# Transposed q and k copied out of PSUM in halves for every pair, in a fused window-attention and mixer kernel

## The chip, the cores and the metric

The kernel runs on one core of a Trainium2 chip. The metric is the device time of one execution in microseconds (us), given as the median over several runs. TensorE is called PE in the profile, VectorE DVE, ScalarE ACT, GpSimd POOL and SyncE SP.

## The reference, cut to what matters

Windowed attention with four sink tokens is followed by a mixer block over tokens and channels. There are 4 batches, 8 heads, 768 positions and head size 64; the mixer's widths are 256 (tokens) and 1536 (channels).

```
scores = scale * np.matmul(q, k.transpose(0, 1, 3, 2))
keep = is_sink | in_window          # first 4 keys, or 0 <= query - key < 128
a = softmax(np.where(keep, scores, -1e9))
x = matmul(a, v)                    # heads side by side: [4, 768, 512]
h = np.maximum(xt @ w_tok1, 0.0) @ w_tok2      # xt: x with tokens last
u = x + h.transpose(0, 2, 1)
out = u + np.maximum(u @ w_ch1, 0.0) @ w_ch2
```

## The kernel before, in words

Work comes in 16 pairs of heads, p = 0 to 15, four of them a batch (`NHP = 4`). For one pair:

- `prepare(p)` (line 393) makes the instructions that copy transposed q and k from PSUM to SBUF, and `transposed(p)` (line 447) is the burst of 24 small PE transposes that fills the PSUM tile they read. The tile has the tag "sc"; its first index x, 0 or 1, separates the first half of the 768 columns from the second, and both q and k have a part in each half. For pairs 0 to 4 q and k are copied in two halves of 384 columns each, from tiles of the tag "mx" (`turn`, line 429). For pairs 5 to 15 each is one copy of 768 columns from the "sc" tile.
- `cleared` (line 470) then zeroes a part of that tile for its next use, on DVE.
- `scores(p, g)` (line 499) multiplies q and k for three groups g, ACT takes the exponential (line 539), and DVE applies a mask (line 547).
- `sink_values(p)` (line 628) opens two PSUM tiles of the tag "mx", one for each head i, and `values(p, i)` (line 662) adds the window's part with 11 matmuls a head. `recip` and `norm` (lines 645 to 653) divide by the sum, both on DVE, and so empty the tile.

For a batch the mixer runs `mix_h` and `mix_u` (tokens), `turned_u` (transposes of u) and `mix_channels` (channels). In `mix_channels` a unit `v1` is four matmuls of 384 columns with w_ch1 into one "mx" tile, emptied by a relu on ACT or DVE (lines 135 and 137), and a unit `out_part` is three matmuls of 512 columns with w_ch2; four of these share one "mx" tile, which is emptied by an addition on DVE (line 924).

PSUM has two tiles of the tag "sc" and four of the tag "mx" (`TAGS`, line 68). A unit on PE that needs a tile takes the one that its readers left first.

The order of all instructions is written out ahead of time by a planner (`Plan`, line 247). PE takes the channel mixing of batch b as its main list, and the attention and token mixing of batch b+1 as a side list. `MERGED` (line 47) gives the merge by hand: "28/48" means that the side list's unit 28 comes once 48 units of the main list are placed. The planner then places the copies, relus and other work on ACT and DVE at the moment at which its own costs say an engine can begin them. Where two of them can begin at the same moment on the same engine, the one with the larger `urgent` goes first, and otherwise the earlier one in the list. In this planner a copy out of PSUM depends on the transposes and on who used its destination before. The planner does not know that one PSUM tile is read by one engine at a time: the tile framework adds such a wait between ACT and DVE by itself when the program is built.

Loads of q, k and v are issued by POOL (lines 107 and 115), stores of the output by SP (line 930).

Of the kernel before, what the change touches and what calls it, by code (L numbers as in the profile page):

```python
# [16 lines left out]
def kernel(  # L17
# [23 lines left out]
    NHP = H // 2  # L41
# [3 lines left out]


    MERGED = (
# [5 lines left out]
    )  # L53
    NQ = 6
    NPT = 3
# [18 lines left out]
    def bank(tag, *shape, dtype=FP32, slot=None):  # L74

        n = given[tag].pop(0) if slot is None else slot
        if tag == "sc":
            return sc[n]
        return psum.tile([P, *shape], dtype, name=f"ps_{tag}", tag=f"{tag}{n}", bufs=1)
# [41 lines left out]
    def mm(*args, **kwargs):  # L121
        in_order(nc.tensor.matmul(*args, skip_group_check=True, **kwargs))  # L122
# [4 lines left out]
    def copy(e, out, in_):  # L127
        if e == "ACT":
            in_order(nc.scalar.activation(out, in_, AF.Copy))  # L129
        else:  # L130
            in_order({"DVE": nc.vector, "POOL": nc.gpsimd}[e].tensor_copy(out=out, in_=in_))  # L131
# [10 lines left out]
    done = {}  # L142
    tiles = {}
# [50 lines left out]
    for n in range(4):  # L194
        i, odd = n // 2, n % 2
# [190 lines left out]
    def piece(ns, fn, deps, need, then, keys=()):  # L386
        op = Op({}, fn, deps, then, size=float(ns))
        op.need, op.keys = need, keys
        return op
# [3 lines left out]
    def prepare(p):  # L393

        kT = kTb[p % NKB]
        parts = 2 if p <= NHP else 1

        def evict(e, n, part):
            name = ("q", "k")[n]
            if n:  # L400
                t = kT
            elif ("qT", p) in tiles:
                t = tiles["qT", p]
            else:
                t = tiles["qT", p] = att_pool.tile([P, S], BF16, name="qT2")
            to = t.rearrange("d (x p j) -> d x p j", x=2, j=NT)
            copy(e, to if parts == 1 else to[:, part], tiles["ps_" + name, p] if parts == 1 else tiles["ps_" + name, p][part])

        free = ([("sk", p - 2)] if p >= 2 else [], [(n, p - NKB) for n in ("s", "sk")] if p >= NKB else [])
        if parts == 2:  # L410
            cost = {"DVE": 540.0, "ACT": 500.0}
        else:
            cost = {"DVE": 950.0} if p < NHP else {"DVE": 950.0, "ACT": 900.0}
        for n, name in enumerate(("qT", "kT")):
            done[name, p] = [
                Op(dict(cost), lambda e, n=n, part=part: evict(e, n, part), free[n]) for part in range(parts)
            ]
            for part, op in enumerate(done[name, p]):
                op.urgent = (3 - part) * (p < NHP)
        tiles["kT", p] = kT  # L420
# [26 lines left out]
    def transposed(p):  # L447

        def run():
            ps = turned_bank(p)  # L450
            for n in range(2):
                for j in range(NT):
                    for x in range(2):
                        rows = ds(D * x, D)
                        in_order(nc.tensor.transpose(ps[:, x, n, j], bfs[p, n][rows, j], ident[rows, rows]))  # L455
                tiles["ps_" + "qk"[n], p] = ps[:, :, n].rearrange("d x j p -> d x p j")

        then = [*done["qT", p], *done["kT", p]]
        then.append(cleared(p, then))
        return piece(  # L460
            350, run, [done["q_bf", p], done["k_bf", p]], {"sc": [then]}, then, [("tq", p), ("tk", p)],
        )

    def turned_bank(key):

        tiles["ps_turned", key] = bank("sc")
        t = tiles["ps_turned", key].bitcast(BF16).rearrange("d x n b c -> d x n (b c)")[:, :, :, 2 * D:8 * D]
        return t.rearrange("d x n (j p) -> d x n j p", j=NT)

    def cleared(key, readers):  # L470

        op = Op(
            {"DVE": 400.0}, lambda e: in_order(nc.vector.memset(tiles["ps_turned", key][0:D, :, :, 3], 0.0)), readers,
        )
        op.urgent = 2
        return op
# [151 lines left out]
    def sink_values(p):  # L628

        b, hp = pairs[p]  # L630
        vsk = v_sinks[p % NHP]

        def run():
            for i in range(2):
                tiles["ps_o", p, i] = bank("mx", NT, D1)
            for qt in range(2, NT):
                for i in range(2):
                    rows = ds(D * i, D)
                    mm(
                        tiles["ps_o", p, i][:, qt], tiles["pT_sink", p][rows, ts(qt - 2, P)], vsk[rows, i],  # L640
                        start=(qt == 2), stop=False,
                    )

        for i in range(2):
            def recip(e, i=i):
                r = tiles["recip", p, i] = pt_pool.tile([P, NT, 1], FP32, name="recip")
                in_order(nc.vector.reciprocal(r, tiles["ps_o", p, i][:, :, D:D1]))

            def norm(e, i=i):
                in_order(nc.vector.tensor_tensor(  # L650
                    out=x_sb[b][:, :, ds((2 * hp + i) * D, D)], in0=tiles["ps_o", p, i][:, :, 0:D],
                    in1=tiles["recip", p, i].to_broadcast([P, NT, D]), op=ALU.mult,
                ))

            done["r", p, i] = Op({"DVE": 180.0}, recip)
            done["x", p, i] = Op({"DVE": 550.0}, norm, [done["r", p, i]])
            done["r", p, i].urgent = done["x", p, i].urgent = 3
        return piece(
            120, run, [done["p", p, NT], done["vs", p]], {"mx": [[done[n, p, i] for n in "rx"] for i in range(2)]}, [],
        )  # L660
# [185 lines left out]
    def attention_and_tokens():  # L846

        parts, units = [], []
        first, last = NHP, len(pairs) - 1
        prepare(first)  # L850
        units += [turn(first, n) for n in range(2)]
        for p in range(first, last + 1):
            b, hp = pairs[p]
            pieces = []
            if p < last:
                prepare(p + 1)
                pieces.append(transposed(p + 1))
            pieces.append(scores(p, 0))
            if p > first:
                pieces.append(sink_values(p - 1))  # L860
            if p == last:
                pieces.append(turned_u(b, 0, "sc"))
            units.append(burst(*pieces))
            if p > first:
                units += [values(p - 1, i) for i in range(2)]
            pieces = [scores(p, 1), scores(p, 2)]
            if hp == 0 and p > first:
                units.append(mix_h(b - 1, 1, 0, NTOK))
                units += [mix_u(b - 1, 1, st, 2) for st in range(0, NT, 2)]
                pieces.append(turned_u(b - 1, 1))  # L870
            if hp == NHP - 1 and p < last:
                pieces.append(turned_u(b, 0))
            if hp % 2 == 0:
                pieces.append(score_sinks(p + 1))
            units.append(burst(*pieces))
            units[-1].then.append(sink_rows(p))
            if hp == 2:
                units.append(mix_h(b, 0, 0, NTOK))
                units += [mix_u(b, 0, st, 2) for st in range(0, NT, 2)]
            if hp == 0 and p > first:  # L880
                parts.append(units)
                units = []
        units += [pv(p, half) for half in range(2)]
        units.append(mix_h(b, 1, 0, NTOK))
        units += [mix_u(b, 1, st, 2) for st in range(0, NT, 2)]
        units.append(burst(turned_u(b, 1)))
        return parts + [units]
# [166 lines left out]
    parts = attention_and_tokens()  # L1054
# [40 lines left out]
```

## Time and profile before

| | us |
|---|---|
| median of 3 runs (lowest to highest) | 206.93 (206.88 to 207.99) |
| the profiled execution | 206.41 |
| its span, first to last instruction | 204.6 |
| PE busy | 197.6 (97%) |
| ACT busy | 113.8 (56%) |
| DVE busy | 112.4 (55%) |
| POOL busy | 67.3 (33%) |
| mean granted PE clock | 1.00 |

The profiled execution is 1.8 us longer than the span of its instructions. A busy share counts the time in which at least one instruction of an engine ran; matmuls are pipelined, so PE's share is high even where it pauses for a few tenths of a microsecond. What limits PE from moment to moment is seen in the order of time, in the stretch of the timeline around a wait.

### The profile page before, as it was taken

The page shows a single profiled execution, that of the slowest core. Times are in us where ns is not written, and L with a number is a line of the kernel's source. Part 1 is how long each engine was busy: PE and PEld are TensorE (multiplying, and loading weights), DVE is VectorE, ACT ScalarE, POOL GpSimd, SP SyncE. Part 2 cuts the span into 40 slices and gives each one's busy share as a digit, 9 for nine tenths or more (in the row PEclk, how much of TensorE's full clock was granted, in tenths as well). Part 3 has the DMA queues.
Part 4 walks back from the last instruction along what each step waited for, and adds up shares of the span by engine and source line. Part 5 has one row for each costly group of instructions (what it writes and reads, how often), then busy time and mean ns, then how long its engine had stood idle before and what let it go on. Part 6 is the DMA issues. An engine that isn't in the chain of part 4 may idle for free.

```text
span 204.6 us, 5496 instructions
## 1 busy us (share of the span) xinstructions
PE 197.6 (97%) x2377; PEld 119.3 (58%) x2377; DVE 112.4 (55%) x238; ACT 113.8 (56%) x195; POOL 67.3 (33%) x86
## 2 busy tenths in 40 slices
PE   6798999999999999999999999999999999999994
PEld 2345985566665665667656545666655645665453
DVE  4775653657788766866948557572654361001222
ACT  4898668879706535886563145886750114773000
POOL 6299859795699891450000000000000000000000
DMA  6999999999999999193001112100002112000223
GB/s 193 292 257 188 169 177 191 160 172 206 157 180 189 187 184 198 22 128 20 3 0 54 53 64 97 51 5 0 0 3 103 51 54 103 0 3 0 103 103 103
DMA packets 73223, 21.58 MB, mean 105 GB/s; under 512 B 63216, under 2 KB 70256, under 8 KB 73200
## 3 DMA queue, kind: packets, MB, share of 16 engines
q0 software_dynamic: 67232, 11.80, 73.1%
q1 hardware_dynamic: 5968, 9.45, 13.1%
q8 instruction: 18, 0.29, 0.6%
q14 instruction: 5, 0.04, 0.1%
HBM read 26.75 MB, written 6.29 MB: 161 GB/s over the span
## 4 chain that ended last, share of the span: by engine, by line
PE 85%; DMA 6%; DVE 3%; ACT 2%; POOL 1%; issue 1%; SPq 0%; POOLq 0%; ACTq 0%
PE ps_mx L122 77%; PE ps_sc L122 4%; DMA w_tok<-in_moe_w_tok_dram 4%; DMA v_sink_f<-in_v_dram 2%; PE ps_sc L455 2%; POOL v_aug L115 1%; DVE kT L131 1%; PE ps_mx L427 1%; ACT pT L539 1%; ACT qT L129 1%; PE ps_mx L125 1%; SPq L197 0%; ACT uT L129 0%; DVE u_sb L751 0%; DVE x_sb L650 0%
## 5 line engine op out<-in xcount | busy, mean ns | idle before, releaser
L122 PE MATMUL ps_mx<-uT,w_ch 128*128 128x384 bf16 x384 | 67.1, 326 | 0.1
L122 PE MATMUL ps_mx<-w_ch,v1T 128*128 128x512 bf16 (+2 forms) x312 | 66.9, 363 | 0.0
L539 ACT ACTIVATE pT<-ps_sc 128x1024 bf16<-128x1024 f32 (+1 forms) x48 | 44.4, 952 | 13.0 <-PE ps_sc L122 12.9
L122 PEld LDWEIGHTS <-w_ch 128*128 128x128 bf16 x384 | 36.0, 98 | 23.9 <-issue 1.2
L135 ACT ACTIVATE v1T<-ps_mx 128x384 bf16<-128x384 f32 x77 | 37.7, 490 | 19.5 <-PE ps_mx L122 18.9
L122 PEld LDWEIGHTS <-v1T 128*128 128x128 bf16 x312 | 28.3, 98 | 27.6 <-issue 0.5
L924 DVE TENSOR_TENSOR o_sb<-ps_mx,u_sb 128x512 f32<-128x512 f32 x23 | 15.8, 687 | 34.6 <-PE ps_mx L122 34.6
L122 PEld LDWEIGHTS <-w_tok 128*128 128x128 bf16 x192 | 18.3, 98 | 5.9 <-DMA w_tok<-in_moe_w_tok_dram 0.7
L107 POOL DMA_DIRECT2D q_bf<-in_q_dram x24 | 19.6, 822 | 4.4 <-DMA w_ch<-in_moe_w_ch_dram 2.2
L107 POOL DMA_DIRECT2D k_bf<-in_k_dram x24 | 19.6, 820 | 4.1 <-DMA w_ch<-in_moe_w_ch_dram 1.7
L751 DVE TENSOR_TENSOR u_sb<-ps_mx,x_sb 128x512 bf16<-128x512 f32 x20 | 13.2, 687 | 13.0 <-PE ps_mx L122 12.9
L115 POOL DMA_DIRECT2D v_aug<-in_v_dram x16 | 16.4, 1026 | 8.3 <-ACT v_sink L129 7.1
L131 DVE COPY kT<-ps_sc 128x768 bf16<-128x768 bf16 x11 | 10.5, 958 | 13.4 <-ACT qT L129 13.4
L122 PEld LDWEIGHTS <-pT 128*128 128x128 bf16 x352 | 14.1, 98 | 3.3 <-issue 0.6
L129 ACT ACTIVATE qT<-ps_sc 128x768 bf16<-128x768 bf16 x11 | 8.9, 810 | 12.3 <-PE ps_sc L455 12.1
L122 PE MATMUL ps_mx<-v_aug,pT 128*128 128x65 bf16 x352 | 15.6, 194 | 0.0
L547 DVE TENSOR_TENSOR pT<-pT,mask_main 128x1024 bf16<-128x1024 bf16 (+1 forms) x24 | 14.3, 619 | 1.3 <-ACT pT L539 1.3
L122 PE MATMUL ps_sc<-qT,kT 64*64 64x192 bf16 (+3 forms) x288 | 14.4, 248 | 0.0
L135 ACT ACTIVATE h1T<-ps_mx 128x512 bf16<-128x512 f32 (+1 forms) x8 | 4.1, 517 | 17.1 <-PE ps_mx L122 16.9
L122 PE MATMUL ps_mx<-h1T,w_tok 128*128 128x256 bf16 x96 | 13.2, 273 | 0.0
L137 DVE TENSOR_SCALAR v1T<-ps_mx 128x384 bf16<-128x384 f32 x19 | 10.4, 549 | 4.9 <-PE ps_mx L122 4.9
L122 PE MATMUL ps_mx<-x_sb,w_tok 128*128 128x256 bf16 x96 | 12.0, 273 | 0.5 <-DMA w_tok<-in_moe_w_tok_dram 0.4
(68 smaller groups left out, 156.6 us busy)
## 6 DMA issues: line engine op xcount, KB each, us to landing
out_dram<-o_sb SPq DMA_DIRECT2D x23, 256.0 KB, 2.0
v_aug<-in_v_dram POOLq DMA_DIRECT2D x16, 192.0 KB, 7.2
w_ch<-in_moe_w_ch_dram POOLq DMA_DIRECT2D x8, 384.0 KB, 8.8
q_bf<-in_q_dram POOLq DMA_DIRECT2D x24, 96.0 KB, 6.8
k_bf<-in_k_dram POOLq DMA_DIRECT2D x24, 96.0 KB, 5.9
q_f<-in_q_dram SPq DMA_DIRECT2D x4, 384.0 KB, 5.0
k_f<-in_k_dram SPq DMA_DIRECT2D x4, 384.0 KB, 5.7
w_tok<-in_moe_w_tok_dram POOLq DMA_DIRECT2D x2, 384.0 KB, 7.7
```

The lines of the kernel that those rows point to most:

```text
L107: in_order(nc.gpsimd.dma_start(out=out[:, h], in_=rows[:, h]))
L115: in_order(nc.gpsimd.dma_start(out=v_aug.rearrange("p i t d -> p (i t) d")[:, :, 0:D], in_=v[b].rearrange("h s d -> (h s) d")[2 * hp * S:2 ...
L122: in_order(nc.tensor.matmul(*args, skip_group_check=True, **kwargs))
L129: in_order(nc.scalar.activation(out, in_, AF.Copy))
L131: in_order({"DVE": nc.vector, "POOL": nc.gpsimd}[e].tensor_copy(out=out, in_=in_))
L135: in_order(nc.scalar.activation(out, in_, AF.Relu))
L137: in_order(nc.vector.tensor_scalar_max(out=out, in0=in_, scalar1=0.0))
L455: in_order(nc.tensor.transpose(ps[:, x, n, j], bfs[p, n][rows, j], ident[rows, rows]))
L539: in_order(nc.scalar.activation(part(tiles["pT", p][:, :, ds(2 * g, 2)]), of_keys(tiles["ps_s", p, g])[:, :, 0:width(g)], AF.Exp, scale=scale,
L547: in_order(nc.vector.tensor_tensor(out=pt, in0=pt, in1=m, op=ALU.mult))
L751: in_order(nc.vector.tensor_tensor(out=u_part(b, g, s0, n), in0=tiles["ps_u", b, g, s0], in1=x_sb[b][:, s0:s0 + n, c0:c0 + cn], op=ALU.add,))
L924: in_order(nc.vector.tensor_tensor(out=o_sb.rearrange("p (g c) -> p g c", g=2), in1=u_rows(b, st), in0=tiles["ps_out", b, st].rearrange("p ...
```

## The change

Three edits. First, the copies of transposed q and k are made in two halves of 384 columns for all pairs, where pairs 5 to 15 had one copy of 768 columns each. Second, `transposed` hands out the two halves of its PSUM tile one by one. Third, the order number `urgent` of the reciprocal and the normalisation in `sink_values` is 2 in place of 3, which is the number that `cleared` has. The list `MERGED` is another one, with the same 75 units of the side list.

```
     MERGED = (
-        "1/0 0/2 2/4 3/8 4/15 5/17 6/17 7/19 8/24 9/25 10/25 11/27 12/27 13/29 14/29 15/30 16/32 17/32 18/35 "
-        "19/36 20/38 21/38 22/38 23/41 25/42 26/42 24/42 27/44 28/48 29/50 31/52 30/52 32/56 33/57 34/57 "
-        "35/60 36/61 39/63 40/63 41/65 42/67 38/67 37/67 43/71 44/76 45/76 46/76 47/80 50/82 48/82 49/82 "
-        "51/86 52/92 53/95 54/95 55/95 56/100 57/102 58/102 59/105 60/106 62/115 67/115 63/115 61/118 64/120 "
-        "65/121 66/128 68/130 69/131 70/133 71/135 72/135 73/135 74/138"
+        "0/0 1/3 2/5 3/10 4/17 5/17 6/18 7/21 8/24 9/25 10/26 11/27 12/28 14/30 13/30 15/31 16/32 17/33 18/34 "
+        "19/36 20/39 21/39 22/39 23/41 26/42 25/42 24/42 27/44 28/51 29/52 30/53 31/55 32/60 33/60 34/60 "
+        "35/65 36/65 37/68 38/68 39/69 40/72 41/73 42/75 43/75 44/80 45/80 46/80 47/83 48/85 49/86 50/86 "
+        "51/88 52/94 53/97 54/97 55/97 56/102 57/103 58/103 60/108 59/110 63/114 61/115 62/115 64/119 67/124 "
+        "65/127 68/129 66/129 69/130 70/133 73/137 71/137 72/138 74/142"
     )
...
     def prepare(p):
...
-        parts = 2 if p <= NHP else 1
+        parts = 2
...
-                tiles["ps_" + "qk"[n], p] = ps[:, :, n].rearrange("d x j p -> d x p j")
+                tiles["ps_" + "qk"[n], p] = [ps[:, x, n].rearrange("d j p -> d p j") for x in range(2)]
...
-            done["r", p, i].urgent = done["x", p, i].urgent = 3
+            done["r", p, i].urgent = done["x", p, i].urgent = 2
```

## The prediction, made before the changed kernel ran

> **What bounds the kernel now.** I read the page's busy shares first, then PE's waits, then the groups of instructions by shape, then the timeline around one pair, and last the chain that ended last.
>
> ```profile
> PE 197.6 (97%) x2377; PEld 119.3 (58%) x2377; DVE 112.4 (55%) x238; ACT 113.8 (56%) x195; POOL 67.3 (33%) x86
> ```
>
> PE is busy for 97% of the span at a granted clock of 1.00 in every stretch, and the two copying engines for little over half. A change that leaves PE's matmuls alone can save only pauses of PE, and can add some. Consecutive matmul starts that lie over 0.1 us further apart than usual, and are not one of PE's regular changes between 64-row and 128-row work, occur after 30 us at four places alone: 70.13 (0.21 us), 72.31 (0.20), 89.86 (0.10) and 98.36 (0.23), 0.74 us together. So little can be won; the question is what new pauses come.
>
> The rows of the copies, with their single durations and what DVE waited for:
>
> ```profile
> L131 DVE COPY kT<-ps_sc 128x768 bf16<-128x768 bf16 x11 | 10.5, 958 | 13.4 <-ACT qT L129 13.4
> L129 ACT ACTIVATE qT<-ps_sc 128x768 bf16<-128x768 bf16 x11 | 8.9, 810 | 12.3 <-PE ps_sc L455 12.1
> L129 ACT ACTIVATE kT<-ps_mx 128x384 bf16<-128x384 bf16 x6 | 2.9, 505 | 0.7 <-PE ps_mx L439 0.6
> L129 ACT ACTIVATE qT<-ps_mx 128x384 bf16<-128x384 bf16 x6 | 2.8, 489 | 0.8 <-PE ps_mx L439 0.6 <-ACT pT L539 0.2
> L131 DVE COPY qT<-ps_mx 128x384 bf16<-128x384 bf16 x4 | 2.2, 554 | 1.2 <-PE ps_mx L439 1.1
> L131 DVE COPY kT<-ps_mx 128x384 bf16<-128x384 bf16 x4 | 2.2, 553 | 1.1 <-PE ps_mx L439 1.1
> L650 DVE TENSOR_TENSOR x_sb<-ps_mx,recip 128x384 bf16<-128x384 f32 x22 | 11.5, 549 | 0.1
> ```
>
> The first row carries the argument: for all 11 pairs k's copy on DVE waits for q's copy on ACT, though it needs nothing of it. The two engines read one PSUM tile in turn. The timeline of pair 6 shows the same in order of time (start, duration):
>
> ```profile
> 42.92 0.28 PE L122 MATMUL ps_mx<-v_sink,pT_sink 64*128 64x65 bf16 x8
> 42.97 0.81 ACT L129 ACTIVATE qT<-ps_sc 128x768 bf16<-128x768 bf16 x1
> 43.14 1.47 PE L122 MATMUL ps_mx<-uT,w_ch 128*128 128x384 bf16 x8
> 43.81 0.96 DVE L131 COPY kT<-ps_sc 128x768 bf16<-128x768 bf16 x1 [2.10 <-ACT qT L129]
> 44.00 0.49 ACT L135 ACTIVATE v1T<-ps_mx 128x384 bf16<-128x384 f32 x1 [0.22 <-PE ps_mx L122]
> 44.38 1.02 ACT L539 ACTIVATE pT<-ps_sc 128x1024 bf16<-128x1024 f32 x1
> 44.45 0.83 PE L122 MATMUL ps_mx<-v_aug,pT 128*128 128x65 bf16 x22
> 45.12 1.46 PE L122 MATMUL ps_mx<-uT,w_ch 128*128 128x384 bf16 x8
> ```
>
> From here come the sizes used below. A unit of four w_ch1 matmuls takes (44.45 - 43.14)/2 = 0.65 us; 11 matmuls of `values` take (45.12 - 44.45)/2 = 0.34; w_ch1 begins 0.17 after ACT's first copy. The hand-off from ACT to DVE is 43.81 - 43.78 = 0.03. Two independent instructions on ACT or DVE overlap by about 0.1 and 0.08 us. And in the chain, the pause at 98.36 is this copy's queue too: q, k, the zeroing and a relu, one after the other, until PE goes on 0.06 us after the relu.
>
> ```profile
> 96.05 0.82 ACT qT L129
> 96.90 0.97 DVE kT L131
> 97.86 0.11 issue
> 97.97 0.27 DVE ps_sc L473
> 98.25 0.46 DVE v1T L137
> ```
>
> **The change part by part.** *PE's work.* The built program has the same 2377 matmuls, and the same 74 changes between 64-row and 128-row work: no term. POOL's list is the same and SP stores in the same order, so transfers move only as PE's steps do, and POOL is idle after 90 us. Up to 30 us all engines' lists agree.
>
> *The halves.* The built program still lets one engine at a time read the tile. Its waits make a chain of four: ACT copies q's first half, DVE waits for it and copies q's second, ACT waits for that and copies k's first half, and DVE waits again and copies k's second. (For pairs 9, 11 and 13 ACT makes both halves of k.) By the rows: 0.49 + 0.55 + 0.51 + 0.55 and three hand-offs of 0.03 make 2.19 us, where 0.81 + 0.03 + 0.96 = 1.80 stood. The chain ends 0.39 us later, and engine time rises by 0.18 us a pair on ACT and 0.15 on DVE, 2.0 and 1.6 us over 11 pairs, which engines that are 56% busy hide. What costs is the place in the queue: ACT's instruction for k now stands ahead of exponential and relus and waits for DVE, and DVE's stands ahead of the normalisation and waits for ACT. Scores themselves do not wait, as those of the pair come several us later.
>
> *The merge.* What matters is how many "mx" tiles PE needs before these queues give one back. `sink_values` holds two of the four until the normalisation; w_ch1 units take one each 0.65 us. Under w_ch2 four units share a tile for 2.6 us, so pairs 7, 8, 9, 12 and 13 have cover; pair 14 has two such units first; pair 5 has no `values` open; at pair 11 the second k half is not on DVE and normalisation goes early. There remain pairs 6, 10 and 15. Before, two w_ch1 units went ahead of `values` there, and ACT's relu right after q's copy (44.00 to 44.49) gave the first tile back in time. Now only one or none goes ahead, and that relu stands behind k's half and the exponential.
>
> With zero at the start of q's first half: DVE q to 1.07, ACT k to 1.61, DVE k to 2.19.
> - Pair 6: `values` 0.17 to 0.51, a unit to 1.16, `values` to 1.50, a unit to 2.15, and the third unit needs a tile at 2.15. The normalisation (0.55, after k's half on DVE, overlap 0.08) ends at 2.66; ACT's exponential (1.02) and relu (0.49) end at 2.92. PE resumes at 2.66 + 0.06 = 2.72: **0.57 us**.
> - Pairs 10 and 15: a unit, both `values` and a second unit, then a third at 2.15, which gets the first unit's tile (relu right behind k on ACT, to 2.00). The fourth wants one at 2.80. DVE after k: reciprocal 0.17, zeroing 0.27 (begins 0.12 after the copy, as at 97.97), normalisation 0.55, overlapping 0.08 each where independent: 3.05, and PE at 3.11: **0.30 us each**.
>
> Bounds: with no hand-offs and each copy at 0.49 to 0.55 the three sum to about 0.9; with 0.12 at each hand-off, the largest such gap in the rows (the zeroing behind k), 0.27 more at each of three places, 2.0. I take 1.17, since the 0.03 of ACT to DVE is the same kind of step.
>
> *What goes.* The pause at 98.36 (pair 12) falls under w_ch2 now, and the one at 89.86 (pair 11) has both `values` and so the normalisation earlier: 0.33 us saved; by the bounds between 0 and 0.33. Those at 70.13 and 72.31 wait for a normalisation and a relu of token mixing, and the order there is nearly the same: 0, from -0.2 to +0.1.
>
> *`urgent`.* With 2 in place of 3 a normalisation and a zeroing that could begin together go in list order; in the built lists the zeroing (0.27) goes ahead of one at pairs 10 and 15, which is in their sum. At pair 6 it goes behind.
>
> Sum: 0.57 + 0.60 - 0.33 = +0.84 us. The profiled execution would take 206.41 + 0.84 = 207.25; the median shown lies 0.52 above it, so the median would be 207.8. About 0.5%, 1.0 us, is what a measurement of this kernel can tell from no change, and the forecast stays just inside it.
>
> **The rivals.**
> - *Halves side by side.* If the two halves of the tile were read at once, ACT's q with DVE's q and then k likewise, the chain would end at 2 x 0.55 + 0.03 = 1.14 in place of 1.80, the normalisation at pair 6 at 1.6, before 2.15, and no new pause comes: 206.93 - 0.33 and at most 0.4 for the other two places, 206.2 to 206.6, not slower. It decides when k's second half on DVE ends before 1.6. For it: the halves are separate parts of the tile. Against it: the 13.4 us of waiting behind ACT, and the same waits between halves in the built program. The Trainium skill, "PSUM — Partial Sum Buffer", section on PSUM bank collisions, says that ScalarE and VectorE may use different banks at once and need guarding by bank (and quadrant) alone; by that rule such waits are not needed between halves in different banks, and the time would be this rival's. The trace does not show two such reads at once.
> - *More places pause.* The layout leaves PE little room elsewhere: pairs 5, 11 and 14 meet w_ch1 units too, and a step from DVE back to ACT inside a tile has no row. At 0.12 a step and two or three places more of 0.3: 0.84 + 0.8 + 0.6, so 208.3 to 209.2. For it: ACT's queue now waits in the middle at eight pairs. Against it: ACT and DVE are idle over 40% of the time.
> - *Nothing to see.* DVE and ACT catch up sooner than laid out, since the planner may have placed relus on the other engine: pauses of 0.3 as gone, 206.6 to 207.1.
>
> **How the numbers follow.** Forecast 0.59 (207.2 to 208.3, centre 207.8; of this 0.11 lies above 207.96), halves side by side 0.07, more places 0.24, nothing to see 0.10. Under 205.9, faster by over 0.5%, lies part of the first rival with an error in the other pauses: 0.05. Slower by over 0.5%: 0.11 + 0.24 = 0.35. Between them: 0.48 + 0.10 + 0.02 = 0.60. The range reaches from the middle of the first rival, 206.5, to 208.9 inside the second.
>
> **What would show it.** In the changed profile: DVE's q and k halves each idle behind ACT and ACT's k half behind DVE, 2.2 us from the first start to the last end; at pairs 6, 10 and 15 (near 46, 85 and 136 us) PE held by the normalisation for 0.6, 0.3 and 0.3 us; no pause at pair 12. The forecast is wrong if halves of ACT and DVE overlap in time, if a copy of 384 columns from the "sc" tile takes much longer than 0.49 to 0.55 us, or if PE is held at other pairs.

## The result, and the profile after

The changed kernel takes 207.74 us (median of 22 runs, 207.00 to 208.93), and the kernel before, run beside it as often, 206.99 (206.11 to 208.12). The ratio is 1.0033, 95% interval 1.0019 to 1.0047: 0.75 us by the medians, slower by less than the 0.5% of the forecast's bound. The interval, 0.4 to 1.0 us, does not hold zero, so the slowdown is real though small. The forecast was 207.8.

The profiled execution of the changed kernel took 208.09 us, with a span of 206.3 and a granted clock of 0.998. Against 206.41 that is 1.68 us more, twice what the medians differ by. Half of it has nothing to do with the change: up to the last of the 128-row transposes of the first batch's u, all engines' lists are the same, and that one starts at 30.03 us before and at 30.82 after, 0.79 us of scatter between two executions. From there to the end the kernel before takes 174.61 us and the changed one 175.49: **+0.88 us**. This stretch is used for all comparisons of traces below.

The busy shares after, from the page:

```profile
PE 198.2 (96%) x2356; PEld 120.0 (58%) x2377; DVE 109.0 (53%) x240; ACT 118.5 (57%) x215; POOL 67.3 (33%) x86
```

Nothing changed its place as the bound. The 2377 weight loads are there; 21 of the matmuls have left no record, so a gap in the matmuls counts as a pause only where the weight loads or a waiting row show it too. The copies from the "sc" tile after, among the groups of instructions by shape (count, then busy us, mean ns of one, then idle time before them and what ended it):

```profile
L129 ACT ACTIVATE kT<-ps_sc 128x384 bf16<-128x384 bf16 x14 | 6.5, 490 | 6.9 <-DVE qT L131 6.9
L131 DVE COPY qT<-ps_sc 128x384 bf16<-128x384 bf16 x11 | 6.1, 558 | 15.0 <-ACT qT L129 15.0
L129 ACT ACTIVATE qT<-ps_sc 128x384 bf16<-128x384 bf16 x11 | 5.4, 491 | 9.9 <-PE ps_sc L455 9.7
L131 DVE COPY kT<-ps_sc 128x384 bf16<-128x384 bf16 x8 | 4.5, 558 | 4.4 <-ACT kT L129 4.4
```

All three rows with a wait between engines name the half that was copied just before on the other one. DVE's wait for q has grown to 15.0 us, from 13.4 for k before, and ACT has a wait of 6.9 us for DVE that it did not have. The counts of 14 and 8 for k are the 11 pairs, with three more for ACT and three fewer for DVE: at pairs 9, 11 and 13 ACT copies both halves of k.

The chain that ended last, at pair 6 (start, length, what), is the predicted chain of four:

```profile
45.06 0.50 ACT qT L129
45.56 0.02 issue
45.58 0.57 DVE qT L131
46.15 0.02 issue
46.18 0.50 ACT kT L129
46.68 0.02 issue
46.70 0.56 DVE kT L131
47.26 0.48 DVE x_sb L650
47.73 0.05 issue
47.78 1.47 PE ps_mx L122 x8
```

From 45.06 to 47.26 it takes 2.20 us. The normalisation begins only behind DVE's last half, and PE goes on 0.05 us after it. What PE was doing meanwhile stands in the timeline of the same stretch:

```profile
45.57 0.81 PE L122 MATMUL ps_mx<-uT,w_ch 128*128 128x384 bf16 x4
46.22 0.50 PE L122 MATMUL ps_mx<-v_aug,pT 128*128 128x65 bf16 x11
46.56 1.02 ACT L539 ACTIVATE pT<-ps_sc 128x1024 bf16<-128x1024 f32 x1
46.57 0.81 PE L122 MATMUL ps_mx<-uT,w_ch 128*128 128x384 bf16 x4
47.17 0.55 DVE L650 TENSOR_TENSOR x_sb<-ps_mx,recip 128x384 bf16<-128x384 f32 x1
47.78 0.50 PE L122 MATMUL ps_mx<-uT,w_ch 128*128 128x384 bf16 x2 [0.40 <-DVE x_sb L650]
```

Two units of w_ch1 go ahead, the third finds no "mx" tile. It begins 0.57 us late (the row's 0.40 counts from the modelled end of the last matmul). Pairs 10 and 15 go alike, with the zeroing between; this is pair 10:

```profile
84.81 0.56 DVE L131 COPY kT<-ps_sc 128x384 bf16<-128x384 bf16 x1 [0.56 <-ACT kT L129]
85.29 0.18 DVE L647 RECIPROCAL recip<-ps_mx 128x6 f32<-128x6 f32 x1
85.52 0.27 DVE L473 MEMSET ps_sc<- 64x256 f32 x1
85.71 0.53 DVE L650 TENSOR_TENSOR x_sb<-ps_mx,recip 128x384 bf16<-128x384 f32 x1
86.30 0.82 PE L122 MATMUL ps_mx<-uT,w_ch 128*128 128x384 bf16 x4 [0.16 <-DVE x_sb L650]
```

The view of PE's waits names the same cause for the whole execution (total us, times, longest):

```profile
PE ps_mx L122 <- DVE x_sb L650: 0.7, 3, 0.4
```

The kernel before has no such row; its pause of 0.21 us at 70.13 ends with a normalisation too, but is too short for this view. Measured by matmul starts, all pauses of 0.1 us or more after 30 us are:

| | before | after |
|---|---|---|
| pair 6 | none | 0.57 at 47.05 |
| pair 10 | none | 0.32 at 85.81 |
| pair 15 | none | 0.32 at 136.51 |
| token mixing | 0.21 and 0.20 | 0.14 and 0.20 |
| pairs 11 and 12 | 0.10 and 0.23 | none |
| together | 0.74 | 1.55 |

They differ by 0.81 us, against 0.88 for the stretch.

### The profile page after: what moved, and what is told of

Read it like the earlier page. It is cut to its first block, busy times and chain, and to the rows that moved or that the text cites. A ratio compares the mean times of both kernels' runs of the same rounds, so it can differ in the third digit from the quotient of the medians.

```text
span 206.3 us, 5502 instructions
## 1 busy us (share of the span) xinstructions
PE 198.2 (96%) x2356; PEld 120.0 (58%) x2377; DVE 109.0 (53%) x240; ACT 118.5 (57%) x215; POOL 67.3 (33%) x86
## 4 chain that ended last, share of the span: by engine, by line
PE 83%; DMA 6%; DVE 4%; ACT 2%; POOL 1%; issue 1%; SPq 0%; POOLq 0%
PE ps_mx L122 75%; PE ps_sc L122 4%; DMA w_tok<-in_moe_w_tok_dram 4%; DMA v_sink_f<-in_v_dram 3%; PE ps_sc L455 2%; PE ps_mx L427 1%; POOL v_aug L115 1%; DVE qT L131 1%; DVE kT L131 1%; ACT qT L129 1%; ACT v1T L135 1%; ACT kT L129 1%; DVE x_sb L650 1%; PE ps_mx L125 1%; SPq L197 0%
## 5 line engine op out<-in xcount | busy, mean ns | idle before, releaser
L122 PE MATMUL ps_mx<-w_ch,v1T 128*128 128x512 bf16 (+2 forms) x294 | 66.1, 362 | 1.2 <-issue 0.5
L135 ACT ACTIVATE v1T<-ps_mx 128x384 bf16<-128x384 f32 x85 | 41.3, 493 | 16.2 <-PE ps_mx L122 15.4
L122 PE MATMUL ps_sc<-qT,kT 64*64 64x192 bf16 (+3 forms) x288 | 15.1, 253 | 0.0
L131 DVE COPY qT<-ps_sc 128x384 bf16<-128x384 bf16 x11 | 6.1, 558 | 15.0 <-ACT qT L129 15.0
L122 PE MATMUL ps_mx<-h1T,w_tok 128*128 128x256 bf16 x96 | 13.4, 273 | 0.0
L122 PEld LDWEIGHTS <-kT 64*64 64x64 bf16 (+2 forms) x320 | 7.9, 102 | 6.9 <-issue 4.4
L650 DVE TENSOR_TENSOR x_sb<-ps_mx,recip 128x384 bf16<-128x384 f32 x22 | 11.7, 547 | 0.2
L129 ACT ACTIVATE qT<-ps_sc 128x384 bf16<-128x384 bf16 x11 | 5.4, 491 | 9.9 <-PE ps_sc L455 9.7
```

Of the source, the lines that this page charges most:

```text
L135: in_order(nc.scalar.activation(out, in_, AF.Relu))
L650: in_order(nc.vector.tensor_tensor(out=x_sb[b][:, :, ds((2 * hp + i) * D, D)], in0=tiles["ps_o", p, i][:, :, 0:D], in1=tiles["recip", p, i ...
```

## The experiments

The theory of the prediction says that the halves make a chain that is handed between ACT and DVE, that this chain stands ahead of the normalisation, and that at three pairs PE runs out of "mx" tiles meanwhile. Each expectation names the theories that it weighs against it. Times are set against the kernel before on the same chip: 206.78 us for the experiments with four halves on ACT, with whole copies, with the new merge alone and with the halves alone, 206.84 for the others; in brackets behind a ratio stands its 95% interval. "The stretch" is the time from the last 128-row transpose to the end: 174.61 us before, 175.49 in the changed kernel.

**All four halves on ACT at the three pairs.** The hand-offs go, the halves, the merge and `urgent` stay:

```
             done[name, p] = [
-                Op(dict(cost), lambda e, n=n, part=part: evict(e, n, part), free[n]) for part in range(parts)
+                Op({"ACT": 500.0} if p in (6, 10, 15) else dict(cost),
+                   lambda e, n=n, part=part: evict(e, n, part), free[n]) for part in range(parts)
             ]
```

> The changed kernel, but at pairs 6, 10 and 15 all four halves are copied by ACT, so that no copy there waits for the other engine and DVE is left to the normalisation. Theory 1 (the chain of four halves that passes between ACT and DVE holds the normalisation, and so PE, at these three pairs): DVE normalises right behind its reciprocal, the three pauses of 0.57, 0.32 and 0.32 us go, and no new one comes: about 1.0 us less than the changed kernel, 0.3 less than before, ratio to before 0.9985. Theory 2 (the price is engine time and the number of instructions, 0.33 us a pair more): ACT gets 0.9 us more at each of the three pairs with relus behind it, and the time stays at the changed kernel's ratio of 1.0033 or rises. Theory 3 (the new merge asks for tiles too early, whatever the copies do): the pauses stay, 1.0033.

Measured: 206.62 us, ratio 0.9992 (0.9974 to 1.0009), stretch 174.30. All three pauses are gone, and those of 0.14 and 0.20 near 71 and 73 us are left. The stretch is 1.19 us shorter than in the changed kernel; the three pauses had been 1.21. Its timeline at pair 6:

```profile
44.97 0.87 ACT L129 ACTIVATE qT<-ps_sc 128x384 bf16<-128x384 bf16 x2
45.69 0.20 DVE L648 RECIPROCAL recip<-ps_mx 128x6 f32<-128x6 f32 x1 [1.98 <-PE ps_mx L122]
45.73 0.88 ACT L129 ACTIVATE kT<-ps_sc 128x384 bf16<-128x384 bf16 x2
45.92 0.56 DVE L651 TENSOR_TENSOR x_sb<-ps_mx,recip 128x384 bf16<-128x384 f32 x1
46.48 1.79 PE L122 MATMUL ps_mx<-uT,w_ch 128*128 128x384 bf16 x10
```

DVE no longer has a copy ahead of the normalisation, which ends at 46.48, 1.51 us after q's copy began (2.66 in the changed kernel), and w_ch1 runs on. That the same halves on one engine cost nothing shows that the halving itself is free at these pairs; what costs is that it is handed to and fro ahead of the normalisation. The theory holds, and the others named there fall.

**Whole copies at the three pairs.**

```
+    WHOLE = (6, 10, 15)
...
-        parts = 2
+        parts = 1 if p in WHOLE else 2
...
-                tiles["ps_" + "qk"[n], p] = [ps[:, x, n].rearrange("d j p -> d p j") for x in range(2)]
+                tiles["ps_" + "qk"[n], p] = ps[:, :, n].rearrange("d x j p -> d x p j") if p in WHOLE else [ps[:, x, n].rearrange("d j p -> d p j") for x in range(2)]
```

> The changed kernel, but at pairs 6, 10 and 15 q and k are one copy of 768 columns each, as before. Theory 1, by the order of the built program and the durations of the rows: the pauses at pairs 10 and 15 go or fall under 0.1 us; at pair 6 one of 0.5 us stays, because there DVE's reciprocal and the zeroing go ahead of the normalisation behind k's whole copy. About 0.4 us less than the changed kernel, ratio to before 1.001. If the halves alone are the cause, all three pauses go: 0.9985. If the merge alone is the cause, all three stay: 1.0033.

Measured: 207.26 us, ratio 1.0025 (1.0006 to 1.0044), stretch 174.94. The pause at pair 10 is gone and 0.10 us is left of that at pair 15, but that at pair 6 is 0.57, as long as in the changed kernel:

```profile
44.57 0.81 ACT L130 ACTIVATE qT<-ps_sc 128x768 bf16<-128x768 bf16 x1
45.41 0.96 DVE L132 COPY kT<-ps_sc 128x768 bf16<-128x768 bf16 x1 [2.10 <-ACT qT L130]
46.28 0.18 DVE L648 RECIPROCAL recip<-ps_mx 128x6 f32<-128x6 f32 x1
46.51 0.27 DVE L474 MEMSET ps_sc<- 64x256 f32 x1
46.70 0.53 DVE L651 TENSOR_TENSOR x_sb<-ps_mx,recip 128x384 bf16<-128x384 f32 x1
47.29 1.47 PE L123 MATMUL ps_mx<-uT,w_ch 128*128 128x384 bf16 x8 [0.40 <-DVE x_sb L651]
```

The two copies take 1.80 us, 0.40 less than the four halves, but the zeroing has now slipped ahead of the normalisation and takes the gain back: with `urgent` at 2 for both, the earlier in the list goes first. So pair 6's place in the new merge is too tight for a shared copy of either kind. This is what theory 1 laid out; neither the halves alone (no pause) nor the merge alone (three pauses) would leave just this one.

**The same, with the zeroing last.** One line more on top of the whole copies:

```
-        op.urgent = 2
+        op.urgent = 0
```

> The kernel with whole copies at pairs 6, 10 and 15, and the zeroing of the PSUM tile with the order number 0 in place of 2, so that it goes behind the normalisation where both could begin. If the zeroing of 0.27 us is what kept the pause at pair 6 with whole copies, the pause falls from 0.57 to about 0.25 us there and nothing else moves. If it is the merge alone, it stays at 0.57.

Measured, in a single run: 207.01 us, stretch 174.61, and the pause at pair 6 is 0.23.

```profile
46.68 0.52 DVE L138 TENSOR_SCALAR v1T<-ps_mx 128x384 bf16<-128x384 f32 x1
47.11 0.55 DVE L651 TENSOR_TENSOR x_sb<-ps_mx,recip 128x384 bf16<-128x384 f32 x1
47.81 0.27 DVE L474 MEMSET ps_sc<- 64x256 f32 x1
```

The size came out as expected, by another way: DVE took a relu (L138) ahead of the normalisation, and it was the relu's tile that PE got. With the zeroing behind, a tile comes free 0.34 us sooner (0.57 - 0.23), whichever of the two goes ahead. By this one run the zeroing accounts for 0.34 of the 0.57 us; the other 0.23 stays with the copies and the merge.

**The new merge alone.** Whole copies for all pairs 5 to 15, with the new `MERGED` and `urgent` 2: the edit of the whole copies, with

```
+    WHOLE = range(5, 16)
```

> The new merge and the changed order number, with one copy of 768 columns for q and for k at pairs 5 to 15 as before. Theory 1: a merge fits the copies that it was found for; laid out by the rows' durations, PE is held by normalisations that are late for token mixing near 71 us (1.7 us) and 116 us (1.0 us), and for 0.5 us near 46 and 94 us: 3.3 us more than before, ratio 1.016. Theory 3 (the merge is the cost, and the halves are harmless): between the changed kernel's 1.0033 and 1.005. If the merge is good and the halves are the cost: below 1.000.

Measured: 210.45 us, ratio 1.0176 (1.0145 to 1.0206), stretch 178.12, 3.5 us longer than before. The pauses are 0.57, 1.71, 0.20, 0.57, 1.06 and 0.10, at 47, 72, 75, 95, 116 and 139 us. The four long ones have the places and nearly the sizes that theory 1 laid out, and the time rules out that the merge is the whole cost or is good by itself. PE's waits:

```profile
PE ps_mx L123 <- DVE x_sb L651: 3.3, 4, 1.5
```

**The halves alone.** The old `MERGED` and `urgent` 3, the halves as in the change:

```
-        "0/0 1/3 2/5 3/10 4/17 5/17 6/18 7/21 8/24 9/25 10/26 11/27 12/28 14/30 13/30 15/31 16/32 17/33 18/34 "
+        "1/0 0/2 2/4 3/8 4/15 5/17 6/17 7/19 8/24 9/25 10/25 11/27 12/27 13/29 14/29 15/30 16/32 17/32 18/35 "
...
-            done["r", p, i].urgent = done["x", p, i].urgent = 2
+            done["r", p, i].urgent = done["x", p, i].urgent = 3
```

> Halves for all pairs with the merge and the order number of before. Theory 1: the chain of halves without a merge fitted to it holds PE at scores near 37 us (0.35 us), at token mixing near 55 and 71 us (0.6 us each) and at w_ch1 near 91 and 99 us (0.2 each): 1.6 us more than before, ratio 1.0075. If the merge is the cost and the halves are harmless: 1.000. If the halves are the whole cost of the change: 1.0033.

Measured: 208.82 us, ratio 1.0097 (1.0063 to 1.0130), stretch 176.40, 1.8 us longer than before. Pauses of 0.46, 0.62, 0.78, 0.20, 0.32 and 0.22 us stand at 38, 56, 72, 75, 93 and 101 us; the five that were expected are among them, and the expected ratio of 1.0075 lies in the interval. That the halves are harmless, or the whole cost of the change, falls. The pause at 56 us hides behind one of PE's regular changes between 64-row and 128-row work: from start to start the matmuls take 0.94 us there, and 0.32 at the same place in the kernel before. The rows show what it waits for:

```profile
56.17 0.54 DVE L650 TENSOR_TENSOR x_sb<-ps_mx,recip 128x384 bf16<-128x384 f32 x1
56.77 1.05 PE L122 MATMUL ps_mx<-x_sb,w_tok 128*128 128x256 bf16 x8 [0.55 <-DVE x_sb L650]
```

PE's waits:

```profile
PE ps_mx L122 <- DVE x_sb L650: 1.3, 3, 0.6
```

The pauses add up to 2.60 us, 1.86 over before, which is about the 1.79 us of the stretch. With the experiment ahead of it this says that the two edits are no sum: the halves alone cost 1.8 us, the merge alone 3.5, both together 0.9. The old merge leaves room for whole copies, the new one for halves. In each mismatch PE waits mostly for the same thing, the normalisation: in four pauses with the merge alone (3.91 of 4.21 us) and in three with the halves alone (1.72 of 2.60). The other pauses with the halves end with an exponential (at 38 us) and with relus (at 75 and 101).

**`urgent` 3 in the changed kernel.** Its one edit is the second of the two in the experiment just told.

> The changed kernel with the order number of reciprocal and normalisation at 3 as before. The built order differs at one place alone: at pair 6 the second head's reciprocal goes ahead of the zeroing. The three pauses stay at 0.57, 0.32 and 0.32 us and the span after the common first 30 us is the changed kernel's.

Measured, in a single run: 207.96 us, stretch 175.48 (175.49 in the changed kernel), pauses of 0.57, 0.32 and 0.32 in the same places. In the changed kernel the edit of `urgent` does nothing to the time.

**All four halves on DVE at the three pairs.** As the first experiment, with the other engine:

```
+                Op({"DVE": 540.0} if p in (6, 10, 15) else dict(cost),
```

> The changed kernel, but at pairs 6, 10 and 15 all four halves are copied by DVE. No copy there waits for the other engine, but DVE has 2.0 us of copies. If the hand-offs and the waiting between engines are the cause, the planner knows what DVE does and puts the normalisation between the halves: the three pauses go. By the order of the built program one of 0.4 us comes at scores near 48 us, which wait for the last half: ratio 1.0005. If it is the copies' work ahead of the normalisation, whichever engine waits, the three pauses stay or grow: 1.0033 or more.

Measured: 207.17 us, ratio 1.0020 (1.0008 to 1.0032), stretch 174.86. The three pauses are gone here too, so it is the passing between engines and not ACT's help that makes them go; but the stretch is 0.56 us longer than with ACT, and the ratio is above the expected one. The time went into a new pause of 0.58 us at 47.74, in the scores:

```profile
46.81 0.55 DVE L131 COPY kT<-ps_sc 128x384 bf16<-128x384 bf16 x1
47.27 0.68 DVE L548 TENSOR_TENSOR pT<-pT,mask_first 128x1024 bf16<-128x1024 bf16 x1
47.99 0.27 DVE L474 MEMSET ps_sc<- 64x256 f32 x1
48.32 0.33 PE L122 MATMUL ps_sc<-qT,kT 64*64 64x192 bf16 x8 [0.34 <-DVE ps_sc L474]
```

The planner let normalisations go between the halves, so k's last half ends at 47.36, and the zeroing of the tile, behind a mask, at 48.26. The scores that need the tile start 0.06 us later. The pause was expected near that place, at 0.4; a smaller one of 0.16 appeared at pair 10.

**The kernel before, with both whole copies on ACT.** Its edit, for pairs 5 to 15:

```
-                Op(dict(cost), lambda e, n=n, part=part: evict(e, n, part), free[n]) for part in range(parts)
+                Op({"ACT": 900.0} if p > NHP else dict(cost), lambda e, n=n, part=part: evict(e, n, part), free[n])
+                for part in range(parts)
```

> The kernel before, its merge and its whole copies, but q and k of pairs 5 to 15 are both copied by ACT, so that no copy waits for the other engine. If waiting for the other engine is what delays the normalisations in the kernel before too, the pauses of 0.10 us near 90, 0.23 near 98 and 0.21 near 70 us go, and by the order of the built program one of 0.1 us comes near 101: 0.3 us less, ratio 0.9985. If engine time is the price, ACT gets about 9 us more in all and the ratio is 1.000 or above.

Measured: 206.63 us, ratio 0.9996 (0.9973 to 1.0019), stretch 174.21. The pauses at 70, 90 and 98 us are gone, as expected; one of 0.09 near 102 us, expected at 0.1 near 101, and one of 0.15 at 48, not expected, are new. The stretch is 0.40 us shorter, but the time can't be told from that of the kernel before, and its interval holds the ratio of both theories; only the pauses decide for the first. No kernel here beats it by more than its interval. The best version of the change, halves on ACT at three pairs, takes 0.4% less than the changed kernel by the two ratios and equals the kernel before.

## Why the prediction was right

- *PE's work.* Right: 2377 weight loads as before, PE at a clock of 0.998, no term.
- *The halves.* Right. The four copies and their hand-offs take 2.20 us at pair 6, where 2.19 was laid out. Over all 11 pairs ACT's halves take 0.49 us, DVE's 0.56. The step from DVE back to ACT, which had no row, takes 0.034 to 0.036 us, and ACT to DVE 0.032 to 0.033: the nearest row, 0.03, was the right choice and the upper bound of 0.12 far off.
- *Engine time is hidden.* Right that it does not show in the time, wrong in size: 2.0 us more on ACT and 1.6 more on DVE were laid out, and ACT's busy time rose by 4.7 (113.8 to 118.5) while DVE's fell by 3.4 (112.4 to 109.0). The term left out the three halves of k that ACT took over and eight relus that the planner moved from DVE to ACT (19 to 11 on DVE, 77 to 85 on ACT).
- *The merge.* Right in place and size: pauses of 0.57, 0.32 and 0.32 us against 0.57, 0.30 and 0.30, each ended by the normalisation. (By its own figures, 3.11 - 2.80, the last two should read 0.31.) Right also that pairs 5, 7 to 9 and 11 to 14 have none. Incomplete at pair 6: halves were given as the cause, but whole copies under the new merge pause there as long, with the zeroing in their place. The third unit of w_ch1 comes too early there for either.
- *What goes.* Right: both pauses, 0.33 us. With the old merge the halves leave pauses of 0.32 and 0.22 us at these two pairs (at 93 and 101 us), so it is the merge that takes them away. The pause at 70.13 was to stay, and fell from 0.21 to 0.14, which is inside its bound.
- *`urgent`.* Right: no effect but the order of list, and the experiment shows the same pauses with 3.
- *The sum.* +0.84 us was laid out; the pauses give +0.81, the stretch +0.88, the medians +0.75. The nearness of the medians is partly luck, with an interval from 0.4 to 1.0 us; that of the pauses is not, as each term came out by itself, 0.57, 0.64 for 0.60, and 0.33.

The rivals. *Halves side by side* falls: all copies of one tile that pass to the other engine wait for the one ahead. The 13.4 us of waiting that were held against it could not decide it, as a whole copy reads both parts x of the tile and a half only one. Its chances don't fit either: 0.05 of its 0.07 was laid under 205.9 us, outside its own 206.2 to 206.6. Yet the kernel before does have two such reads at once, from separate "mx" tiles, in its timeline for pair 4:

```profile
30.56 0.49 ACT L129 ACTIVATE kT<-ps_mx 128x384 bf16<-128x384 bf16 x1 [0.64 <-PE ps_mx L439]
30.63 0.55 DVE L131 COPY kT<-ps_mx 128x384 bf16<-128x384 bf16 x1
```

This corrects the prediction's remark that the trace shows no two such reads at once: not from one tile, but from two. The Trainium skill, "PSUM — Partial Sum Buffer", section on PSUM bank collisions, asks for a guard by bank (and quadrant) alone; these two rows agree with it if the two tiles lie in different banks, which no view states. The waits inside the "sc" tile are put there by the tile framework as the program is built. Whether two halves of that tile could be read at once was not tried: it would take the tile apart into separate ones. *More places pause* falls with the pauses listed above and the hand-off of 0.035 us. *Nothing to see* falls, as the three pauses have their full size.

## What to carry to other kernels

Splitting a copy shortens nothing while its halves are handed between engines inside one tile (1.80 us became 2.20 here): it makes more hand-offs, and the time to look at is when the *last* of them ends, and what stands behind it on that engine's queue. A price for such a change comes from laying out one period by row durations and asking at which moment the bounding engine next needs a buffer; that gave each of three pauses here within 0.02 us. A merge written by hand belongs to the copies it was made for, so two edits that cost 1.8 and 3.5 us each can cost 0.9 together, and neither is judged alone.

## What the runs showed that was not expected

- A hand-off back from DVE to ACT is as short as one from ACT to DVE: 0.035 against 0.033 us.
- Giving all four copies of a pair to ACT costs nothing: two halves on ACT overlap by 0.10 us, so the four end 1.64 us after the start (44.97 to 46.61), sooner than the 2.20 of two engines that share them.
- The zeroing of an "sc" tile decides twice: ahead of the normalisation it holds PE for "mx" tiles (whole copies, 0.34 us of the pause of 0.57), and late it holds the scores (halves on DVE, 0.58 us).
